# Halved first q*k products, class-1 norms in portions and a reset of the fill model's TensorE position in a fused attention and token-mixing kernel

## Chip, cores, metric

One core of one Trainium2 chip. The metric is the time of one execution on the device in microseconds (us); medians are over several executions. All bf16 data, float32 sums.

## The reference

Two layers, each run twice: A is attention over eight positions two apart, B is a two-matmul mixer over the 2048 tokens.

```python
S, D, H, W, dil, F = 2048, 1024, 32, 8, 2, 3584          # head size 32
def A(x):                                                # x is already layer-normed
    q, k, v = split(x @ wqkv)                            # 32 heads
    idx = pos[:, None] - arange(W) * dil                 # the window: 8 earlier tokens, 2 apart
    attn = softmax(where(idx >= 0, (q * k[idx]).sum(-1) * Dh**-0.5, -1e9))
    return (attn * v[idx]).sum(window) @ wo
def B(x):
    u = gelu(einsum("bsd,sf->bdf", layernorm(x), w1) + b1)
    return transpose(einsum("bdf,fs->bds", u, w2) + b2)
x = x + A(layernorm(x)); x = x + B(layernorm(x))         # and both once more
```

As the window steps by two, even tokens never meet odd ones. The kernel calls them class 0 and class 1 (`c`); each is 1024 tokens, eight tiles of 128 x 1024.

## The kernel before

The q*k products of the window are made on VectorE (`T`), summed over the head by TensorE with a 0/1 matrix (`sel`), turned into probabilities, written to device memory and read back spread over the partitions (`pb`), and multiplied by v on VectorE. Projections, layer norms of the second class and the output projection are "fill" that keeps TensorE busy meanwhile. A small model of TensorE's and VectorE's positions, run while the kernel is built, decides how many fill groups stand between which steps. The engines themselves run their lists in order (run r37_norm0_first below shows it for VectorE). A fill group is eight matmuls of 512 columns, about 1.75 us.

```python
class Attn:
    def weights(self, c, part, dt):          # part 0 q, 1 k, 2 v; loaded when first asked for
        ...                                  # v: two tiles of 512 KB from a pool of five (wb)
                    nc.sync.dma_start(out=t, in_=src)
    def project(self, c, part, dt, hf, ps=None, lo=0, hi=HT):
        ...                                  # 8 matmuls of hi - lo columns, then a ScalarE copy
    def softmax_back(self, n):
        ...                                  # sums, reciprocal, Pb on VectorE
            nc.gpsimd.dma_start(out=dst, in_=Pb[:].rearrange("p u t -> p (u t)"))   # pd, in device memory
            self.spread(n)
    def spread(self, n):
            for hf in range(2):
                ...
                nc.gpsimd.dma_start(out=pb[:].rearrange("p b u t -> p (b u t)"), in_=src)   # 1 MB each

    def stream(self, lead):                  # the main line of one attention layer; weave() adds fill
            for n in range(last + 1):        # n: chunk of 16 heads of one class
                for half in range(2):
                    yield from self.qk(n, 2 * half)
                    yield from self.qk(n, 2 * half + 1)
                    if half:
                        yield from self.softmax_front()
                    ...

def weave(lead, fills, lags):                # pe, dve: modelled positions in us
    ...
            elif kind == "at":
                pe, dve = unit               # sets both positions to given values

def opening():
    for i in range(NT):
        x_stage(0, i)                        # tiles of class 0, alternating between two queues
    load_biases()
    clear_pads()
    with tc.manual_schedule(...):
        first_tiles(hT, ...)                 # norms, transposes and first projections in a fixed order
        for i in range(NT):
            x_stage(1, i)
    yield "at", 27.0, 29.0
    ...
```

## Time and profile before

| | before |
|---|---|
| time, median of 3 (range) | 1280.47 us (1280.17 to 1280.98) |
| profiled span | 1278.8 us |
| TensorE busy | 98% |
| granted TensorE clock | 1.00 |
| start of the first useful projection | 11.98 us |
| start of the value projections after the first softmax | 63.55 us |

```profile
DMA to landing us min/median/max: 4.9/4.9/4.9
```

### The profile page before, as it was taken

The page shows a single profiled execution, that of the slowest core. Times are in us where ns is not written, and L with a number is a line of the kernel's source. Part 1 is how long each engine was busy: PE and PEld are TensorE (multiplying, and loading weights), DVE is VectorE, ACT ScalarE, POOL GpSimd, SP SyncE. Part 2 cuts the span into 40 slices and gives each one's busy share as a digit, 9 for nine tenths or more (in the row PEclk, how much of TensorE's full clock was granted, in tenths as well). Part 3 has the DMA queues.
Part 4 walks back from the last instruction along what each step waited for, and adds up shares of the span by engine and source line. Part 5 has one row for each costly group of instructions (what it writes and reads, how often), then busy time and mean ns, then how long its engine had stood idle before and what let it go on. Part 6 is the DMA issues. An engine that isn't in the chain of part 4 may idle for free.

```text
span 1278.8 us, 15455 instructions
## 1 busy us (share of the span) xinstructions
PE 1258.0 (98%) x6163; PEld 577.4 (45%) x6284; DVE 689.9 (54%) x869; ACT 489.3 (38%) x812; POOL 61.3 (5%) x166
## 2 busy tenths in 40 slices
PE   8999999999999999999999999999999999999998
PEld 4344444444444444444444444444444444444444
DVE  6789999999114322334798834899930233111011
ACT  6845446634424533324533445453352343000000
POOL 3000000001000000000000000010010000000000
PEclk9999999999999999999999999999999999999999
DMA  9853454553422289952738542358262223344331
GB/s 256 190 124 106 99 139 142 171 143 115 132 83 83 64 220 305 291 161 87 187 103 201 152 124 80 83 159 207 66 181 83 82 67 89 107 128 135 99 115 52
DMA packets 217817, 173.00 MB, mean 135 GB/s; under 512 B 32081, under 2 KB 198353, under 8 KB 215697
## 3 DMA queue, kind: packets, MB, share of 16 engines
q1 hardware_dynamic: 206768, 126.11, 36.5%
q0 software_dynamic: 9248, 37.51, 10.5%
q10 hardware_dynamic: 1728, 8.39, 1.7%
q8 instruction: 49, 0.80, 0.3%
q14 instruction: 24, 0.19, 0.0%
HBM read 139.47 MB, written 26.21 MB: 130 GB/s over the span
## 4 chain that ended last, share of the span: by engine, by line
PE 76%; DVE 5%; issue 2%; ACT 1%; DMA 0%; DVEq 0%
PE ps L719 30%; PE ps L743 29%; PE ps L418 11%; PE ps L664 4%; DVE T L456 2%; PE sc L480 1%; DVE pr L538 1%; DVE pr L543 1%; DVE xr L689 0%; ACT h L227 0%; ACT h L238 0%; DMA wo<-in_A_wo_dram 0%; DVE v L545 0%; DVE xr L692 0%; ACT ln L200 0%
## 5 line engine op out<-in xcount | busy, mean ns | idle before, releaser
L719 PE MATMUL ps<-h,w 128*128 128x512 bf16 x1754 | 385.6, 379 | 4.0 <-ACT h L238 2.0
L743 PEld LDWEIGHTS <-w 128*128 128x128 bf16 x1820 | 177.6, 98 | 209.9 <-issue 2.1
L719 PEld LDWEIGHTS <-w 128*128 128x128 bf16 x1792 | 175.2, 98 | 214.1 <-issue 3.4
L418 PE MATMUL ps<-hT,wq 128*128 128x512 bf16 (+1 forms) x1087 | 240.2, 374 | 2.5 <-issue 0.6
L743 PE MATMUL ps<-g,w 128*128 128x512 bf16 (+1 forms) x1017 | 225.9, 376 | 1.2 <-issue 0.2
L743 PE MATMUL ps<-gg,w 128*128 128x512 bf16 (+1 forms) x766 | 170.9, 376 | 0.9 <-issue 0.2
L418 PEld LDWEIGHTS <-wq 128*128 128x128 bf16 x1112 | 109.1, 100 | 128.8 <-issue 9.1
L748 DVE SCALAR_TENSOR_TENSOR xr<-ps,b_sb,xr 128x512 bf16<-128x512 f32 (+1 forms) x65 | 45.5, 738 | 225.1 <-PE ps L743 182.6
L456 DVE TENSOR_TENSOR T<-q,k 128x4096 bf16<-128x4096 bf16 x44 | 99.0, 2284 | 70.5 <-ACT q L422 52.4
L543 DVE TENSOR_TENSOR pr<-pr 128x2048 bf16<-128x2048 bf16 (+1 forms) x128 | 119.4, 949 | 0.3
L730 DVE TENSOR_TENSOR tmp<-ps,gg 128x512 f32<-128x512 f32 x48 | 33.2, 692 | 150.2 <-PE ps L719 148.2
L418 PE MATMUL ps<-hT,wv 128*128 128x512 bf16 x436 | 99.5, 380 | 0.6
L664 PE MATMUL ps<-wo,oT 128*128 128x512 bf16 x377 | 88.6, 379 | 1.1 <-DVE oT L545 0.7
L425 ACT CAST k<-ps 128x1024 bf16<-128x1024 f32 x60 | 60.7, 1014 | 61.0 <-PE ps L418 59.0
L538 DVE TENSOR_TENSOR pr<-pb,v 128x2048 bf16<-128x2048 bf16 x64 | 75.9, 1218 | 10.8 <-ACT v L425 6.1
L538 DVE TENSOR_TENSOR pr<-pb,g 128x2048 bf16<-128x2048 bf16 x64 | 76.6, 1216 | 7.6 <-DMA pb<-pd 5.1
L418 PEld LDWEIGHTS <-wv 128*128 128x128 bf16 x448 | 48.9, 111 | 48.7 <-issue 4.2
L730 DVE TENSOR_TENSOR tmp<-ps,g 128x512 f32<-128x512 f32 x48 | 33.2, 692 | 49.7 <-PE ps L719 46.9
L664 PEld LDWEIGHTS <-oT 128*128 128x128 bf16 x384 | 37.3, 98 | 46.8 <-issue 1.2
L422 ACT CAST q<-ps 128x512 bf16<-128x512 f32 x60 | 34.9, 586 | 49.5 <-PE ps L418 49.5
L731 ACT ACTIVATE gg<-tmp,b_sb 128x512 bf16<-128x512 f32 x48 | 34.6, 721 | 49.9 <-DVE tmp L730 49.9
L731 ACT ACTIVATE g<-tmp,b_sb 128x512 bf16<-128x512 f32 x48 | 34.6, 721 | 43.5 <-DVE tmp L730 43.1
(97 smaller groups left out, 755.9 us busy)
## 6 DMA issues: line engine op xcount, KB each, us to landing
w<-in_B_w_dram SPq DMA_DIRECT2D x56, 512.0 KB, 4.8
w<-in_B_w_dram SPq DMA_DIRECT2D x64, 448.0 KB, 3.8
wq<-in_A_wqkv_dram SPq DMA_DIRECT2D x38, 512.0 KB, 4.3
pb<-pd POOLq DMA_DIRECT2D x16, 1024.0 KB, 8.7
wo<-in_A_wo_dram SPq DMA_DIRECT2D x16, 512.0 KB, 3.9
xa<-xr POOLq DMA_DIRECT2D x32, 256.0 KB, 3.4
xr<-xa SPq DMA_DIRECT2D x32, 256.0 KB, 4.0
wv<-in_A_wqkv_dram SPq DMA_DIRECT2D x14, 512.0 KB, 5.4
```

Source lines behind the costliest of these rows:

```text
L418: nc.tensor.matmul(ps[:, lo:hi], lhsT=cols, rhs=self.hT[c][hf][:, kt, lo:hi], start=(kt == 0), stop=(kt == KD - 1))
L422: nc.scalar.copy(out=self.q_of(c, dt)[:, hf * HT:(hf + 1) * HT], in_=ps[:])
L425: nc.scalar.copy(out=window(buf, 0, PADK + hf * HT, [(KW + 1, 2), (1, HT)]), in_=ps[:].unsqueeze(1).to_broadcast([P, 2, HT]))
L456: mult = nc.vector.tensor_tensor(out=T, in0=q.unsqueeze(1).to_broadcast([P, 4, SC]), in1=window(k, par, 2, [(2, 4), (1, SC)]), op=ALU.mult)
L538: mult = nc.vector.tensor_tensor(out=pr[:, :, u, :], in0=pb[:, :, u, :], in1=window(self.v_of(c, dt), par, 2 + hf * HT, [(TB, 4), (2, 4), ...
L543: nc.vector.tensor_tensor(out=pr[:, :, 0:wd, :], in0=pr[:, :, 0:wd, :], in1=pr[:, :, wd:2 * wd, :], op=ALU.add)
L664: nc.tensor.matmul(banks[(i, n)][:], lhsT=at_.oT[c][kt][:, i * P:(i + 1) * P], rhs=wo_t[n][kt // 4][:, kt % 4, :], start=(kt == 0), stop=( ...
L719: nc.tensor.matmul(ps[:], lhsT=wt[c][:, i, fl * P:(fl + 1) * P], rhs=h2[c][i // 4][:, i % 4, dc * 512:(dc + 1) * 512], start=(k == 0), sto ...
L730: nc.vector.tensor_tensor(out=tmp[:], in0=ps[:], in1=gs, op=ALU.add)
L731: nc.scalar.activation(out=gs, in_=tmp[:], func=ACT.Gelu_apprx_tanh, bias=b1_sb[:, ft:ft + 1])
L743: nc.tensor.matmul(ps[:, 0:xc.stop - xc.start], lhsT=w2t(ft, c), rhs=g[ft // GF][:, ft % GF, xc], start=(ft == 0), stop=(ft == FT - 1))
L748: nc.vector.scalar_tensor_tensor(out=xo[:, xc], in0=ps[:, 0:xc.stop - xc.start], scalar=b2_sb[:, i, c:c + 1], in1=xo[:, xc], op0=ALU.add, ...
```

## The change

The intent is to start useful TensorE work earlier and to have the first q*k sums ready earlier. Tile 0 comes in two halves on two queues; projections start on 128 columns; three q*k products are made on their first half of the tokens before class 1's statistics (`AHEAD_T`); class 1's norms are spread between the products; its last tile moves from ScalarE to VectorE; and as the projections have moved ahead of the first softmax, the model's positions are set anew there (`39.3, 54.6`).

```diff
+    AHEAD_T = ((0, 0), (0, 1), (1, 0))
...                                          # first_tiles: new order of statistics, norms, transposes, projections
+        for dq, par in AHEAD_T:
+            ahead(0, dq, par, HT)
     def prologue_tile(c, i, hT):
         t = staged(c, i)
-        if i % 2:
+        if i % 2 and i < NT - 1:            # this branch normalises on ScalarE
...
             if lead is not None:
-                yield "drain", "second"
+                for dq, par in AHEAD_T:
+                    self.multiply_ahead(0, dq, par, SC)
+                yield from self.qk(0, 0)
+                for u in ((1, 3, 1), (0, 2, 0)):
+                    yield from self.proj(0, *u)
+                self.multiply_ahead(0, 1, 1, SC)
+                for u in ((0, 2, 1), (0, 3, 0), (0, 3, 1)):
+                    yield from self.proj(0, *u)
+                yield "drain", "second", NT // 2
...
+                    if lead is not None and n == 0:
+                        yield "drain", "second", NT // 4
                     if half:
+                        if lead is not None and n == 0:
+                            yield "at", 39.3, 54.6
                         yield from self.softmax_front()
...
         def opening():
-            for i in range(NT):
-                x_stage(0, i)
-            load_biases()
+            x_stage(nc.sync, 0, 0, slice(0, P // 2))
+            x_stage(nc.scalar, 0, 0, slice(P // 2, P))
+            x_stage(nc.scalar, 0, 1)
+            x_stage(nc.sync, 0, 2)
+            at_.weights(0, 1, 0)
+            x_stage(nc.scalar, 0, 3)
+            x_stage(nc.sync, 0, 4)
+            at_.weights(0, 0, 0)
...                                          # biases load after class 1's tiles
```

More of the change, by code (lines that the diff above doesn't have):

```diff
@@ L139 @@
     sel = const.tile([P, SB * DQ, 32], BF16, name="sel")
+    maskc = const.tile([P, W, W], FP32, name="maskc")
+    b1_bf = const.tile([P, FT], BF16, name="b1_bf")
+    b2_bf = const.tile([P, NT, DIL], BF16, name="b2_bf")
+    b1_sb = const.tile([P, FT], FP32, name="b1_sb")
+    b2_sb = const.tile([P, NT, DIL], FP32, name="b2_sb")
     nc.gpsimd.memset(sel[:], 0.0)
@@ L145 @@
                 nc.gpsimd.memset(sel[hp * DH:(hp + 1) * DH, sb * DQ + dq, col:col + 1], 1.0)
-    maskc = const.tile([P, W, W], FP32, name="maskc")
     nc.gpsimd.memset(maskc[0:CH], 0.0)
@@ L150 @@
             nc.gpsimd.memset(maskc[0:CH, s, 0:w], NEG)
-    b1_bf = const.tile([P, FT], BF16, name="b1_bf")
-    b2_bf = const.tile([P, NT, DIL], BF16, name="b2_bf")
-    b1_sb = const.tile([P, FT], FP32, name="b1_sb")
-    b2_sb = const.tile([P, NT, DIL], FP32, name="b2_sb")
     def load_biases():
@@ L245, in staged, with x_stage, first_tiles @@
         return g[n // GF][:, n % GF, :]
-    def x_stage(c, i):
-        eng = nc.gpsimd if c else (nc.scalar if i % 2 else nc.sync)
-        eng.dma_start(out=staged(c, i), in_=xin_v[c, i])
-    def first_tiles(hT, project):
+    def x_stage(eng, c, i, part=slice(0, P)):
+        eng.dma_start(out=staged(c, i)[part], in_=xin_v[c, i][part])
+    def first_tiles(hT, project, ahead):
         tiles = [staged(0, i) for i in range(NT)]
-        mv, rs, tps = {}, {}, {}
+        bn, mv, rs, tps = {}, {}, {}, {}
         s1, t1, nm, ss = (st(n, [P, w]) for n, w in (("s1", NDC), ("t1", 1), ("nm", 1), ("ss", 1)))
@@ L262, in idle, with stats, root, moments @@
                                  rhs=ident[:].unsqueeze(1).to_broadcast([P, 4, P]), start=True, stop=True)
-        def moments(i):
-            s = st("bn", [P, NDC, 6])
-            for n in range(NDC):
-                nc.vector.bn_stats(out=s[:, n, :], in_=tiles[i][:, n * 512:(n + 1) * 512])
-            mv[i] = st("mv", [P, 2])
-            nc.vector.bn_aggr(out=mv[i][:], in_=s[:])
+        def stats(i, n):
+            if n == 0:
+                bn[i] = st("bn", [P, NDC, 6])
+            nc.vector.bn_stats(out=bn[i][:, n, :], in_=tiles[i][:, n * 512:(n + 1) * 512])
+            if n == NDC - 1:
+                mv[i] = st("mv", [P, 2])
+                nc.vector.bn_aggr(out=mv[i][:], in_=bn[i][:])
+        def root(i):
             rs[i] = st("rs", [P, 1])
             rsqrt(rs[i][:], mv[i][:, 1:2], 1.0, eps1)
+        def moments(i):
+            for n in range(NDC):
+                stats(i, n)
+            root(i)
         def norm(i):
@@ L295, in first_tiles @@
         dve, act = nc.vector.tensor_copy, nc.scalar.copy
-        idle(16)
-        moments(0)
-        own_sum(0)
-        moments(1)
+        idle(14)
+        stats(0, 0)
+        stats(0, 1)
+        root(0)
+        stats(1, 0)
         norm(0)
         turn(0)
+        stats(1, 1)
+        root(1)
+        place(0, act)
+        own_sum(0)
         idle(3)
-        own_sum(1)
-        moments(2)
+        stats(2, 0)
         norm(1)
         turn(1)
-        idle(5)
-        place(0, act)
@@ L309, in first_tiles @@
-        moments(3)
-        place(1, dve)
-        norm(2)
-        norm(3)
-        banks = {}
-        for u, i in (((1, 0), 2), ((1, 1), 3), ((0, 0), None)):
-            banks[u] = bank()
-            project(*u, 0, banks[u], 0, 2 * P)
-            if i:
-                turn(i)
-        own_square()
-        place(2, act)
+        banks = {u: bank() for u in ((1, 0), (1, 1), (0, 0), (0, 1))}
+        for u in ((1, 0), (1, 1)):
+            project(*u, 0, banks[u], 0, P)
+        stats(2, 1)
@@ L321, in first_tiles @@
+        root(2)
+        place(1, act)
+        stats(3, 0)
+        norm(2)
+        turn(2)
+        stats(3, 1)
+        root(3)
+        own_sum(1)
+        own_square()
+        norm_act(tiles[own], tiles[own], nm, rs[own])
+        place(2, dve)
+        for u in ((1, 0), (1, 1)):
+            project(*u, 0, banks[u], P, 2 * P)
+        norm(3)
+        project(0, 0, 0, banks[(0, 0)], 0, 2 * P)
+        turn(3)
+        stats(own + 1, 0)
         place(3, dve)
-        norm_act(tiles[own], tiles[own], nm, rs[own])
@@ L323, in first_tiles @@
-        moments(own + 1)
+        project(0, 1, 0, banks[(0, 1)], 0, 2 * P)
+        stats(own + 1, 1)
+        root(own + 1)
         moments(own + 2)
+        norm(own + 1)
         for n, u in enumerate(banks):
             project(*u, 0, banks[u], 2 * P, HT)
-            if n == 0:
+            if n == 2:
                 turn(own)
-                norm(own + 1)
                 place(own, dve)
-                moments(own + 3)
-                norm(own + 2)
-        for n, u in enumerate(((0, 1), (1, 2), (1, 3))):
-            if n == 2:
-                norm(own + 3)
-            turn(own + 1 + n)
-            place(own + 1 + n, dve)
-            project(*u, 0, bank(), 0, HT)
@@ L339, in first_tiles @@
-        for u in ((1, 0), (1, 1), (0, 0), (0, 1)):
+        moments(own + 3)
+        norm(own + 2)
+        turn(own + 1)
+        place(own + 1, dve)
+        norm(own + 3)
+        project(1, 2, 0, bank(), 0, HT)
+        turn(own + 2)
+        place(own + 2, dve)
+        ps = bank()
+        project(1, 3, 0, ps, 0, 2 * P)
+        turn(own + 3)
+        place(own + 3, dve)
+        project(1, 3, 0, ps, 2 * P, HT)
+        for u in ((1, 0), (0, 0), (1, 1), (0, 1)):
             project(*u, 1, bank(), 0, HT)
+        for dq, par in AHEAD_T:
+            ahead(0, dq, par, HT)
@@ L364, in __init__ @@
             self.prior = None
+            self.begun = {}
         def v_of(self, c, dt):
@@ L417, in project @@
                     cols = wt[0][:, kt, (dt % 2) * P:(dt % 2 + 1) * P]
-                nc.tensor.matmul(ps[:, lo:hi], lhsT=cols, rhs=self.hT[c][hf][:, kt, lo:hi], start=(kt == 0), stop=(kt == KD - 1))
+                self.last_mm = nc.tensor.matmul(ps[:, lo:hi], lhsT=cols, rhs=self.hT[c][hf][:, kt, lo:hi], start=(kt == 0), stop=(kt == KD - 1))
             if hi < HT:
@@ L454, in qk @@
                     yield "pe", 0.6, [], [], 0.0
-                T = self.t_buf(n, dq, par)
-                mult = nc.vector.tensor_tensor(out=T, in0=q.unsqueeze(1).to_broadcast([P, 4, SC]),
-                                               in1=window(k, par, 2, [(2, 4), (1, SC)]), op=ALU.mult)
+                if (n, dq, par) in self.begun:
+                    self.multiply_ahead(n, dq, par, SC)
+                    T, _, mult = self.begun[(n, dq, par)]
+                else:
+                    T = self.t_buf(n, dq, par)
+                    mult = self.multiply(T, q, k, par, 0, SC)
                 Ts.append(T)
@@ L462, in qk @@
                 if not joined:
-                    self.qk_sum(dq, par, T)
+                    mms = self.qk_sum(dq, par, T)
+                    if dq == 1 and par:
+                        follow(mms[0], self.last_mm, mybir.DependencyClass.NoSync)
             if joined:
@@ L468, in qk, with multiply, multiply_ahead @@
                     follow(x, y, mybir.DependencyClass.NoSync)
+        def multiply(self, T, q, k, par, lo, hi):
+            return nc.vector.tensor_tensor(out=T[:, :, lo:hi], in0=q[:, lo:hi].unsqueeze(1).to_broadcast([P, 4, hi - lo]),
+                                           in1=window(k, par, 2 + lo, [(2, 4), (1, hi - lo)]), op=ALU.mult)
+        def multiply_ahead(self, n, dq, par, hi):
+            c, dt = n // NCQ, (n % NCQ) * DQ + dq
+            T, lo, mult = self.begun.get((n, dq, par)) or (self.t_buf(n, dq, par), 0, None)
+            if lo < hi:
+                mult = self.multiply(T, self.q_of(c, dt), self.k_of(c, dt), par, lo, hi)
+            self.begun[(n, dq, par)] = T, hi, mult
         def t_buf(self, n, dq, par):
+            if (self.li, n, dq, par) == (0, 0, 1, 0):
+                return g_two[-1][:].rearrange("p (u t) -> p u t", u=4)
             if self.li == 0 and 0 < n < 3:
@@ L595, in stream @@
                     turn = nx == (NCQ, 0) and self.li > 0
-                    yield from self.qk(n, 2 * half)
+                    if lead is None or n or half:
+                        yield from self.qk(n, 2 * half)
                     yield from self.qk(n, 2 * half + 1)
+                    if lead is not None and n == 0:
+                        yield "drain", "second", NT // 4
                     if half:
+                        if lead is not None and n == 0:
+                            yield "at", 39.3, 54.6
                         yield from self.softmax_front()
-                    if lead is not None and nx == (0, 1):
-                        for u in ((0, 2, 1), (0, 3, 0), (0, 3, 1),):
-                            yield from self.proj(0, *u)
-                    elif nx[0] <= last and not turn:
+                    if nx[0] <= last and not turn and (lead is None or nx != (0, 1)):
                         yield from qk_proj(*nx)
@@ L832, in weave @@
             elif kind == "drain":
-                while unit[0] in opened:
+                for _ in range(unit[1]) if unit[1:] else iter(int, 1):
+                    if unit[0] not in opened:
+                        break
                     pull(True)
@@ L871, in opening @@
         def opening():
-            for i in range(NT):
-                x_stage(0, i)
-            load_biases()
+            x_stage(nc.sync, 0, 0, slice(0, P // 2))
[6 more added lines that the diff above has]
+            at_.weights(0, 0, 0)
+            for i in range(5, NT):
+                x_stage(nc.sync, 0, i)
             clear_pads()
             with tc.manual_schedule(engines={getattr(mybir.EngineType, e) for e in ("PE", "DVE", "Activation", "Pool")}):
-                first_tiles(hT, partial(at_.project, 0))
+                first_tiles(hT, partial(at_.project, 0), at_.multiply_ahead)
                 for i in range(NT):
-                    x_stage(1, i)
+                    x_stage(nc.gpsimd, 1, i)
+                load_biases()
             yield "at", 27.0, 29.0
-            for u in ((1, 2, 1), (1, 3, 1), (0, 2, 0),):
-                yield from at_.proj(0, *u)
+            yield from at_.proj(0, 1, 2, 1)
         def second_class():
```

## The prediction

> **What bounds the kernel now.** I first read the page's busy row, then the chain that ended last, then TensorE's own waits, then the first 64 us engine by engine in order of time.
>
> ```profile
> PE 1258.0 (98%) x6163; PEld 577.4 (45%) x6284; DVE 689.9 (54%) x869; ACT 489.3 (38%) x812; POOL 61.3 (5%) x166
> PE 76%; DVE 5%; issue 2%; ACT 1%; DMA 0%; DVEq 0%
> PE sc L480 <- DVE T L456: 3.4, 9, 1.2
> PE ps L719 <- ACT h L238: 2.0, 2, 1.2
> PE tp L290 <- DVE gg L233: 1.8, 2, 1.2
> ```
>
> TensorE is busy 98% of 1278.8 us and carries 76% of the chain; its named waits sum to about 11 us (the three largest shown: total us, times, longest). So a change outside the matmuls themselves can win a few us at most. The diff touches only the first softmax and what precedes it, so that is where I look:
>
> ```profile
> 1.57 5.30 PE L261 MATMUL ps<-ident 128*128 128x512 bf16 x16 [1.57 <-POOL ident masks.py:199]
> 8.06 0.62 PE L290 MATMUL tp<-ident,gg 128*128 128x128 bf16 x8 [1.19 <-DVE gg L233]
> 8.52 0.81 PE L261 MATMUL ps<-ident 128*128 128x512 bf16 x3
> 9.90 0.62 PE L290 MATMUL tp<-ident,gg 128*128 128x128 bf16 x8 [0.57 <-DVE gg L233]
> 10.36 1.24 PE L261 MATMUL ps<-ident 128*128 128x512 bf16 x5
> 11.98 1.03 PE L418 MATMUL ps<-hT,wq 128*128 128x256 bf16 x8 [0.38 <-ACT t L281]
> ...
> 25.61 7.07 PE L418 MATMUL ps<-hT,wq 128*128 128x512 bf16 x31
> ...
> 39.65 0.61 PE L480 MATMUL sc<-T,sel 128*32 128x512 bf16 x8 [1.24 <-DVE T L456]
> ```
>
> Columns: start, duration, engine, line, what; idle before it in brackets. The 24 products on `ident` compute nothing: they fill time and keep the array's clock up. The first useful projection starts at 11.98. From there to 25.61 TensorE has no gap worth naming (13.47 busy of 13.63). One more gap, 1.24 us, comes at the first q*k sum, which waits for VectorE's product T. Counting the stretch 25.61 to 63.55 (start of the value projections after the first softmax's sums): 144 matmuls of 512 columns at 0.217 (56 of them ran in the 12.19 us to 37.80) are 31.2, 64 sum matmuls at 0.069 (16 take 1.1) are 4.4; 37.9 less 35.6 leaves 2.3 us of stalls.
>
> **What the Trainium skill says.** "TensorE: Matmul & The Clock Gate", section "Wait — 56ns, not 53.3ns?": start-to-start 55.6 ns for 128 columns and 215.7 for 512 when warm, twice that cold. The trace agrees: eight transposes start 0.46 us ahead of what follows (57 ns each), the long stretches run at 217 ns. Sixteen `ident` products took 5.30 us, which solves to about nine cold; so fourteen of them still pass the warm-up, and I expect no cold projections. "VectorE: DVE Perf Modes", section "The perf-mode tier table": a bf16 tensor_tensor of 2048 elements takes 1224 ns. The trace agrees (1218 for 2048, 2284 for 4096); two halves of T cost 0.1 us more than one whole. "DMA: Bandwidth & Descriptors", section "Anatomy of one DMA — SWDGE (gpsimd) path": about 2.0 us fixed plus the bytes. Here a 256 KB tile lands 3.1 us after issue when the engines are free, and 5 to 6 in a crowd. The same page, section "Issuing engines are not separate DMA queues": splitting a load over queues saves only issue time, so halving tile 0 helps only because tile 1 no longer shares its first microsecond.
>
> **The change, part by part.** Durations are from the trace of before; in-order positions are from the built instruction lists of both kernels. All clock times of the new kernel are estimates.
>
> Loading. Tiles 0 and 1 landed at 4.6 to 4.8, when about 0.7 MB had moved. With tile 0 in two halves at the head of two queues, it needs 0.26 MB, which had moved by about 3.1; with the same 0.8 from there to the landing, it lands near 3.95. The first weights move from fifth to third on their queue: 1.5 MB ahead of or beside them at 0.33 MB/us gives 7.5 instead of 10.9.
>
> Tile 0. Two statistics (1.32) and the aggregate (0.2) end at 5.5, the root on ScalarE (0.56) at 6.05. VectorE now does one half of tile 1's statistics, not both and the aggregate, ahead of the normalisation: 6.05 to 6.55 instead of 7.47 to 8.01. Turn 0 starts at 6.6 (was 8.06); fourteen fillers, at 2 x 0.22 less, end at 6.4.
> Tile 1. Statistics end 7.35, root 7.9, normalised 8.45, turn 1 at 8.5 to 8.95 (was 9.90). ScalarE copies hT of tile 0 from 7.9 to 8.85 (was 9.91 to 10.9).
> First projection: 8.95, on 128 columns of tile 0, against 11.98. The five last fillers (1.24) are gone. But turn 2 must wait for tile 2's root, which stands behind the hT copy and a sum on ScalarE: 10.5, while the two 128-column groups end at 9.9. So 0.6 us of the 3.0 is given back. Then hT of tile 1 (10.95), tile 2 (11.85), tile 3 (14.1) and the ScalarE-normalised tile 4 (16.0) are each ready as TensorE arrives; the rest of the opening has the same columns as before. I place the start of the second-half projections at 23.05 against 25.61: 2.55 us won.
>
> Class 1. Its loads are triggered by the last transpose, so they start 1.3 us earlier in the trace's terms (24.35 becomes 23.05), land from 26.15, and no longer meet the two bias loads, which before had the DMA engines over 90% busy at under 100 GB/s about 12 to 15 us. VectorE, in order, does one T half (22.95 to 24.1), then waits for that first tile.
> VectorE from 26.15 without a gap: statistics 1.32, four T halves 4 x 1.14, aggregate and statistics 1.4, half 1.14, whole T 2.22 (ends 36.85); then normalisations of tiles 0, 2 and 4, statistics of tiles 4 and 6, and half of tile 7, which is new on VectorE: 4.9; T of the next channel at 41.8 to 44.05, the remaining tile 7 statistics 0.77, three more T to 51.4.
> TensorE: 80 matmuls and 16 sums from 23.05 reach 41.45, two sum groups 42.55; the next sum waits for 44.05 (1.5 us), the later three wait 0.45, 0.15 and 0.15. That is 2.25 us of stalls, as many as before: the stall moves from one place to another. Sums end at 52.0 (was 59.0), and the value projections start at 61.0 against 63.55. Won: 2.55.
>
> After that. VectorE runs the softmax and the next products some 7 us earlier, TensorE 2.55. From 63.55 to 188 TensorE had no wait, and the reset of the fill model shifts only one or two fill groups between the same waits; total columns are equal. At 188.1 the output projection waited 0.67 for VectorE, at 200.2 a sum 0.3, at 230.8 ScalarE's normalised tile 1.17. VectorE's lead should remove the first and perhaps half of the other two: 1.4 less. From 240 on both kernels are the same and TensorE-bound.
> Sum: 2.55 + 1.4 = 3.95. I hold back 0.75 for waits I have not seen, since every step above sits on hand-placed starts: 3.2 won, 1280.47 - 3.2 = 1277.3.
>
> **Rivals.**
> (a) The VectorE chain is worse than counted. Tile 7's work (2 statistics, aggregate, normalisation: 1.9 us) moves to VectorE ahead of the sums, and VectorE is full from 26 to 51. For it: three sums in a row stand with nothing between them on TensorE. If class-1 tiles land 2 us late (they took up to 6.1 before), TensorE waits 3.5 instead of 1.5 there; 1279.3. Against: they now meet less traffic.
> (b) Tile 0 does not land sooner, because halves of a tile share the same 16 engines. Then all of the opening shifts by 0.65: 1278.0.
> (c) Waits after 188 all vanish and VectorE's lead stays: 2.1 instead of 1.4, nothing held back; 1275.8.
> (d) The opening's gain is eaten wholly by later waits on VectorE, which is 93% busy from 63.55 to 188 and could set the pace there: 1280. Against it: VectorE starts that stretch earlier than TensorE does, and TensorE shows no wait in it.
>
> **Range and chances.** 1275.3 to 1279.3 covers (a) to (c), each alone. The three runs of before lie within 0.8 us. Two per cent is 25.6 us: more than all of TensorE's idle time together, and no step I found could cost as much. Faster 0.005, same 0.99, slower 0.005.
>
> **What would show it right or wrong.** In the changed kernel: tile 0's statistics start near 3.95; first projection near 9.0, with some 0.6 idle ahead of turn 2; second-half projections near 23; the largest wait of the stretch, about 1.5, ahead of the fifth sum group (T on the next channel); last sum near 52; value projections at 61. If the last sum ends near 52 but the end gains nothing, (d) holds. If the fifth sum waits over 3, (a) holds. If I am wrong beyond the range, it will be through a DMA wait in the opening (the second weights, estimated 10.5 to 11 for a need at 11.9) or a fill placed so that the first softmax's ScalarE copy comes late.

## More of the kernel before

A 512 KB load of value weights goes out on the SyncE queue as soon as TensorE has finished with the buffer that it fills, and 1 MB loads of spread probabilities go out on the GpSimd queue. First SyncE's queue, then GpSimd's, in order of time (start and duration of the issue; the bracket is what the issue waited for):

```profile
122.68 0.37 SPq L396 DMA_DIRECT2D wv<-in_A_wqkv_dram  x1
123.54 0.67 SPq L654 DMA_DIRECT2D wo<-in_A_wo_dram  x1
```

```profile
119.20 0.63 POOL L506 DMA_DIRECT2D pd<-Pb  x1 [45.35 <-DVE Pb L502]
124.58 0.51 POOL L520 DMA_DIRECT2D pb<-pd  x1 [4.75 <-DVE pr L538]
130.16 0.51 POOL L520 DMA_DIRECT2D pb<-pd  x1 [5.07 <-DVE pr L538]
```

The weights leave 1.90 us ahead of the first `pb`. TensorE's timeline runs through this stretch without a bracket:

```profile
121.62 15.70 PE L418 MATMUL ps<-hT,wv 128*128 128x512 bf16 x70
```

The weights on tile `wv` took 4.9 us (the line on DMA in this section), so they landed at 127.6.

## The result and the profile after

The changed kernel took 1287.40 us (median of 6, 1283.02 to 1290.54), against 1280.53 (1280.17 to 1281.08) for the kernel before beside it: 6.9 us slower where 3.2 faster was predicted. The ratio is 1.005, with an interval of 1.0033 to 1.0068.

The busy row and the chain, which the prediction read first, hardly move:

```profile
PE 1259.1 (98%) x6188; PEld 579.6 (45%) x6309; DVE 692.4 (54%) x876; ACT 487.1 (38%) x802; POOL 61.5 (5%) x166
PE 75%; DVE 5%; issue 2%; ACT 1%; DMA 0%; DVEq 0%
```

TensorE's waits do (total us, times, longest). The first line is new:

```profile
PE ps L447 <- DMA wv<-in_A_wqkv_dram: 6.4, 1, 6.4
PE sc L527 <- DVE T L505: 4.3, 11, 0.9
```

The opening on TensorE, in order of time; it answers to the timeline in the prediction. "Turn 0" in the prediction and below is its first line, the eight transposes of tile 0; turn 1 is those of tile 1:

```profile
8.21 0.62 PE L299 MATMUL tp<-ident,gg 128*128 128x128 bf16 x8 [0.72 <-DVE gg L235]
...
10.66 1.06 PE L447 MATMUL ps<-hT,wq 128*128 128x128 bf16 x16
...
24.64 7.08 PE L447 MATMUL ps<-hT,wq 128*128 128x512 bf16 x31
...
45.05 0.62 PE L527 MATMUL sc<-T,sel 128*32 128x512 bf16 x8 [0.91 <-DVE T L505]
...
61.86 4.48 PE L447 MATMUL ps<-hT,wv 128*128 128x512 bf16 x19
```

The first projection is 1.3 us earlier, the second-half projections 1.0 earlier, the value projections 63.55 - 61.86 = 1.7 earlier. So the opening does win, though less than predicted. Then TensorE stands at 126:

```profile
118.03 7.93 PE L447 MATMUL ps<-hT,wv 128*128 128x512 bf16 x35
132.31 11.89 PE L447 MATMUL ps<-hT,wv 128*128 128x512 bf16 x43 [6.35 <-DMA wv<-in_A_wqkv_dram]
```

SyncE's queue and GpSimd's at the same place, and the landing time of these weights:

```profile
120.81 0.37 SPq L425 DMA_DIRECT2D wv<-in_A_wqkv_dram  x1
121.67 0.61 SPq L711 DMA_DIRECT2D wo<-in_A_wo_dram  x1
```

```profile
115.61 0.63 POOL L553 DMA_DIRECT2D pd<-Pb  x1 [46.90 <-DVE Pb L549]
121.24 0.51 POOL L567 DMA_DIRECT2D pb<-pd  x1 [5.00 <-DVE pr L585]
126.57 0.51 POOL L567 DMA_DIRECT2D pb<-pd  x1 [4.82 <-DVE pr L585]
```

```profile
DMA to landing us min/median/max: 11.5/11.5/11.5
```

The same 512 KB took 11.5 us instead of 4.9. Its issue comes 1.9 us earlier than before, but the first `pb` comes 3.3 earlier, so the lead shrank from 1.90 to 0.43 us. The need came sooner too: TensorE stood 5.15 us after the issue (125.96 - 120.81). Two runs below that have the fill order of the kernel before, r37_x_first and r37_norm0_first, show when it would have come there: TensorE began its wait for these weights 6.87 and 6.88 us after their issue. So two things got worse at once, and both come from where the fill stands.

The profile also tells whose packets the 16 engines moved from 124 to 128 us: q0 carries GpSimd's loads (`pb`), q1 SyncE's (the value weights and the loads around them); the columns are packets, MB and share of the engines' time. First the changed kernel, then the one before:

```profile
q0 software_dynamic: 110, 0.88, 100.0%
q1 hardware_dynamic: 32, 0.03, 4.0%
```

```profile
q1 hardware_dynamic: 1617, 1.31, 103.1%
q0 software_dynamic: 7, 0.06, 4.0%
```

In the changed kernel the `pb` load had the engines almost to itself while the weights were still missing. Before, the weights' queue had them, and `pb` came after.

There is a second cost. Windows over the stall, after (busy us of each engine, then the granted clock, DMA share, GB/s):

```profile
126.00:130.00 4.00, 0.00 (x0) 0.00 (x0) 4.00 (x4) 0.15 (x1) 0.51 (x1) 1.00 1.02 237
130.00:132.00 2.00, 0.00 (x0) 0.00 (x0) 2.00 (x2) 0.00 (x0) 0.00 (x0) 0.50 1.15 256
132.00:134.00 2.00, 1.69 (x4) 0.59 (x5) 2.00 (x2) 0.00 (x0) 0.00 (x0) 0.50 1.04 220
134.00:136.00 2.00, 2.00 (x6) 0.73 (x5) 0.95 (x2) 1.02 (x1) 0.00 (x0) 0.50 0.32 71
136.00:138.00 2.00, 2.00 (x9) 0.87 (x8) 0.00 (x0) 0.61 (x1) 0.00 (x0) 0.79 0.04 16
138.00:140.00 2.00, 2.00 (x11) 1.08 (x10) 0.00 (x0) 1.29 (x2) 0.00 (x0) 1.00 0.00 0
```

The array's clock halved while it stood, and came back after 136. That is as the Trainium skill has it ("TensorE: Matmul & The Clock Gate", section "What's actually happening"): half rate after an idle window of about 3.4 us, and full rate again after about as long of work. Here it halved 4.0 us into the wait (at 130.0) and was back 4.5 us after the work began (at 136.8). The 43 matmuls after the stall took 11.89 us; the run pb_late below did 44 there in 9.69, of which one matmul is 0.2, so the cold clock cost about 2.4.

The sum: 6.35 + 2.4 - 1.7 = 7.05 us slower. The second part of the output projection starts at 221.20 us, before at 214.13: 7.07 later. The spans differ by 6.7, the medians by 6.9; at 746 us the kernel before idles 0.44 for no wait that the profile shows, and the changed one does not. So the stall and its cold clock account for the loss to within 0.4 us.

### The profile page after: what moved, and what is told of

Same layout as the page of the kernel before. It is cut to its first block, busy times and chain, and to the rows that moved or that the text cites. A ratio compares the mean times of both kernels' runs of the same rounds, so it can differ in the third digit from the quotient of the medians. Undisturbed runs are those within 1.5% of the kernel's fastest.

```text
span 1285.5 us, 15502 instructions
## 1 busy us (share of the span) xinstructions
PE 1259.1 (98%) x6188; PEld 579.6 (45%) x6309; DVE 692.4 (54%) x876; ACT 487.1 (38%) x802; POOL 61.5 (5%) x166
## 4 chain that ended last, share of the span: by engine, by line
PE 75%; DVE 5%; issue 2%; ACT 1%; DMA 0%; DVEq 0%
PE ps L776 29%; PE ps L800 29%; PE ps L447 11%; PE ps L721 4%; DVE T L505 2%; PE sc L527 1%; DVE pr L585 1%; DVE pr L590 1%; DVE xr L746 1%; ACT h L229 0%; ACT h L240 0%; DMA hT<-hb 0%; DVE xr L749 0%; ACT ln L202 0%; DVE v L592 0%
## 5 line engine op out<-in xcount | busy, mean ns | idle before, releaser
L447 PE MATMUL ps<-hT,wq 128*128 128x512 bf16 (+2 forms) x1112 | 239.8, 370 | 1.8 <-issue 0.3
L505 DVE TENSOR_TENSOR T<-q,k 128x4096 bf16<-128x4096 bf16 (+1 forms) x45 | 97.2, 2193 | 70.4 <-ACT q L451 52.0
L447 PE MATMUL ps<-hT,wv 128*128 128x512 bf16 (+1 forms) x443 | 101.6, 382 | 6.9 <-DMA wv<-in_A_wqkv_dram 6.4
```

Of the source, the lines that this page charges most:

```text
L447: self.last_mm = nc.tensor.matmul(ps[:, lo:hi], lhsT=cols, rhs=self.hT[c][hf][:, kt, lo:hi], start=(kt == 0), stop=(kt == KD - 1))
L505: return nc.vector.tensor_tensor(out=T[:, :, lo:hi], in0=q[:, lo:hi].unsqueeze(1).to_broadcast([P, 4, hi - lo]), in1=window(k, par, 2 + lo ...
```

## Experiments

**1. pb_late: take the collision away.** The changed kernel, with the two `pb` loads of that chunk held until the value weights have landed.

```diff
-            self.spread(n)
+            if (self.li, n) != (0, 1):
+                self.spread(n)
...
-                nc.gpsimd.dma_start(out=pb[:].rearrange("p b u t -> p (b u t)"), in_=src)
+                pb_load = nc.gpsimd.dma_start(out=pb[:].rearrange("p b u t -> p (b u t)"), in_=src)
+                if load:
+                    follow(pb_load, load, mybir.DependencyClass.Sync)
...
+                        if (self.li, n) == (0, 1):       # after the value projections' weights are asked for
+                            self.spread(n, self.last_load)
```

> The changed kernel, where only the two loads of the spread probabilities of the second chunk (2 MB in all) wait until the value weights that TensorE stalled on at 125.9 us have landed; every engine's list is otherwise the same. Theory 1, the two loads share the 16 DMA engines and the probabilities squeeze the weights: issued at 120.8, the weights land in 4 to 5 us as in the kernel before, the 6.35 us stall and the half-clock stretch after it go, span about 1285.5 - 6.4 - 2.2 = 1277, time 1278 to 1279, steady to 1 us. Theory 2, the fill order releases and uses that weight buffer too close together, whatever else is in flight: the stall stays at 4 us or more and the time above 1283.

Measured: 1279.56 us (1279.02 to 1280.12), ratio to before 0.9988 [0.9973, 1.0002], so 7.8 us under the changed kernel. The `pb` loads now go out at 127.28, the weights take 6.2 us, and the stall is down to what the early need leaves (5.16 us after the issue):

```profile
126.78 9.69 PE L447 MATMUL ps<-hT,wv 128*128 128x512 bf16 x44 [1.10 <-DMA wv<-in_A_wqkv_dram]
185.73 11.40 PE L726 MATMUL ps<-wo,oT 128*128 128x512 bf16 x52 [0.87 <-DVE oT L595]
```

The collision is the cause of the stall, all but the 1.10 us that the early need leaves. Holding the probabilities back 6 us brought no other new wait.

**2. reset37: move the model's position alone.** `"at", 39.3, 54.6` becomes `"at", 37.6, 54.6`. The built lists then have the fill order of the kernel before from the first softmax on.

> The changed kernel with the fill model's TensorE position set to 37.6 instead of 39.3, one fill unit (1.75 us) earlier, which gives TensorE the fill order of the kernel before from the first softmax on. Theory 1 (collision, set by how far VectorE leads and by the lead time from release to use): use comes 1.5 us later after release, so the stall shrinks but does not vanish unless the probability loads also come later; 0 to 4.5 us, time 1278.5 to 1285. Theory 2 (fill order alone): no stall, time 1278 to 1279.

Measured: 1280.28 us (1279.90 to 1281.47), ratio 0.9995 [0.998, 1.001]. The weights go out at 121.94, 1.56 ahead of `pb`, land 6.2 later, and there is no stall. So a shift of 1.7 us in a number that only places fill is worth 7 us here.

**3. no_reset: the changed kernel without the reset.**

```diff
-                        if lead is not None and n == 0:
-                            yield "at", 39.3, 54.6
```

> The changed kernel without the reset of the fill model's position. The model then believes TensorE to be later and puts fewer class-1 value units early, so that some are left behind the third softmax and the output projection is split around the sums. If the reset is what brings the weights' release and use together, the 6.35 us stall is gone; but TensorE waits longer for VectorE before the output projection and after it, by 2 to 5 us: 1280 to 1285. If the reset does not matter, the stall and about 1287 stay.

Measured: 1285.92 us (1282.61 to 1286.62), ratio 1.0036 [1.0019, 1.0053]. The weights' stall is 0.29, but other waits come up, by TensorE's timeline:

```profile
97.02 1.05 PE L527 MATMUL sc<-gg,sel 128*32 128x512 bf16 x16 [1.38 <-DVE gg L505]
101.42 1.05 PE L527 MATMUL sc<-gg,sel 128*32 128x512 bf16 x16 [1.29 <-DVE gg L505]
133.96 2.78 PE L447 MATMUL ps<-hT,wv 128*128 128x512 bf16 x12 [0.29 <-DMA wv<-in_A_wqkv_dram]
191.83 3.78 PE L719 MATMUL ps<-wo,oT 128*128 128x512 bf16 x10 [2.61 <-DMA wo<-in_A_wo_dram]
```

After the last of these the granted clock was 0.50 from 192.5 to 195.9 us. A reset is needed, then; it is its value that put the fill in a bad place. The first `pb` load went out 6.04 us ahead of the weights here (119.66 and 125.70), and the weights took 8.2 us; the stall is small only because the need, too, came 8 us after the issue. So going out behind `pb` is slow as well.

**4. before_collide and before_collide2: bring the collision into the kernel before.** The weights' load is made to wait, first for a VectorE product, then for the landing of the write of `pd`.

```diff
+                    load = nc.sync.dma_start(out=t, in_=src)
+                    if (self.li, key, n) == (0, (0, 2, 1), 1):
+                        follow(load, self.pb_free, mybir.DependencyClass.Sync)    # before_collide
+                        follow(load, self.pd_write, mybir.DependencyClass.Sync)   # before_collide2
```

> The kernel before, where the same value weights wait for the VectorE product that also releases the first probability load, so that they are issued together at 124.5 instead of 1.9 us ahead of it. Theory 1: the weights land some 11 us later, at about 135.5 to 136, TensorE stalls 6 us from 129.5 and runs some us at half clock; time 1286 to 1290. Theory 2: they land in 5 us, at 129.4, just in time; time within 1 us of the kernel before.

Measured: 1280.32 us (1280.09 to 1280.57), ratio 0.9993 [0.9979, 1.0008]. A miss of the experiment: the product was done before the wait could hold anything, the weights went out at 122.84 against `pb` at 124.61. It tells nothing.

> The kernel before, where the value weights that it loads at 122.7 us wait for the landing of the probabilities' write, which is what the first probability load of the second chunk waits for too; so both are issued together near 124.6 (the earlier try at this missed: its wait was over before it bit, and the weights still led by 1.8 us). TensorE needs them near 129.5. Collision theory: they land 10 to 11.5 us after issue, at 135 to 136, TensorE stalls 5.5 to 6.5 us and then runs some 4 us at half clock; 1286 to 1290. Fill-order theory (the lead time from release to use, 5 us, is what matters): they land in 5 to 6 us, stall 0 to 1 us, time within 1.5 us of the kernel before.

Measured: executions of 1280.46, 1287.70, 1289.46 and 1287.86 us, ratio 1.0047 [1.0018, 1.0075]. The profile caught the 1280.46: weights out at 124.07, `pb` at 124.61, landing after 5.6 us, no stall. In the other three the kernel before is as slow as the changed one. So one program falls either way; its lead was 0.54 us in the execution that got off free, and is not known for the others. That the slow three stalled as in the changed kernel is inferred from their time and from the granted clock (0.997, as in the changed kernel, against 1.00); no trace shows it.

**5. pb_2k: smaller rows.** I suspected that the `pb` load's rows of 8 KB starve the weights' rows of 1 KB. The Trainium skill ("DMA: Bandwidth & Descriptors", section "Queues, rings and completion order") says that each DMA engine goes round the queues and drains a whole packet of one before the next. Each `pb` load of that chunk becomes four with rows of 2 KB.

```diff
+                parts = 4 if (self.li, n) == (0, 1) else 1
+                for m in range(parts):
+                    size = 4 * W * TB // parts
...
+                    nc.gpsimd.dma_start(out=pb[:].rearrange("p b u t -> p (b u t)")[:, m * size:(m + 1) * size], in_=src)
```

> The changed kernel with each of the two probability loads of the second chunk issued as four, of 2 KB rows instead of 8 KB rows; same bytes. If a row of one queue is taken in turn with a row of the other, weights of 1 KB rows get a third of the engines instead of a ninth: they land in about 5 to 7 us instead of 11.5, the stall falls from 6.35 to under 2 us and the clock is not lost; time 1278 to 1281. If the engines are shared by bytes, or the loads are simply too many, the stall stays about 6 us and the time about 1287.

Measured: 1284.37 us (1281.98 to 1289.04), ratio 1.0019 [1.0, 1.0037]; in the profiled execution (the slowest) the weights took 10.6 us and TensorE stalled 5.53. That landing and that stall fit the second theory, but the share of the engines fits the first: q1, the weights' queue, had 30.9% of the engines' time from 125 to 129 us, near the third reckoned with, against the 4.0% above. And the lead was 0.01 us here, not 0.43. So smaller rows gave the weights more of the engines but did not save this landing; what they would do at the same lead is not shown, and the other three executions (1281.98 to 1285.41) have no trace. The rate fell as well, from 344 and 340 GB/s (124 to 126, 126 to 128 us) before to 236 and 222 in the changed kernel, at a DMA share above 1.0 in both. That is the rate of the `pb` load itself: alone on the engines in the kernel before, from 130 to 134 us, it moved 0.89 MB, 222 GB/s, at a share of 100.0%.

**6. r37_x_first: is the opening short because of the load order?** On top of reset37, the first weights go behind tiles 2 and 4 on their queue.

```diff
-            at_.weights(0, 1, 0)
             x_stage(nc.scalar, 0, 3)
             x_stage(nc.sync, 0, 4)
+            at_.weights(0, 1, 0)
             at_.weights(0, 0, 0)
```

> The changed kernel with the fill position at 37.6 and, in the opening, the first two weight loads behind tiles 2 and 4 on their queue instead of between them; all engine lists but the DMA queue's are as in the run with 37.6 alone. Theory: turn 0 starts at 8.2 to 9.0 instead of the predicted 6.6 because VectorE stands, in order, at tile 1's statistics until tile 1 lands at 7.0, its rows being shared with the weights' 512-byte rows. Then tile 1 lands near 5, turn 0 starts near 6.9, the first projection near 9.2 and the end gains 1.0 to 1.5 us on 37.6 alone: about 1279. Rival: the first megabyte simply moves more slowly whatever its order; turn 0 stays over 8 and the time within 0.5 of 37.6 alone.

Measured: 1280.97 us (1279.74 to 1283.07), ratio 1.0006 [0.9991, 1.0021]. Turn 0 came at 9.14, tile 1 landed at 7.9, no better than reset37 (8.52 and 7.3). The order is not it.

**7. r37_x_first_tile7: the last class-1 tile back on ScalarE** (`if i % 2:`), on top of run 6.

> The same with tile 7 of class 1 normalised on ScalarE as in the kernel before. Theory: the 1.3 to 1.9 us of VectorE work ahead of the third channel's product is what TensorE waits for at the fifth sum group (0.9 to 1.7 us there); without it that wait falls by 0.6 to 1.3 us, and the end gains as much if no other wait takes its place. Rival: the product then waits for ScalarE's copy of the projection, since ScalarE has the tile's three passes (3 us) back; the wait stays.

Measured: 1279.28 us (1278.43 to 1286.61), ratio 1.0004 [0.9976, 1.0031]. The fifth sum waits 1.97 (1.74 in reset37), but the 0.34 at the sixth is gone, and three of the four executions are 1278.4 to 1279.5. The fourth, 1286.61, has the size of the stall, although the profiled execution issued the weights 1.94 us ahead of `pb` (landing after 6.6 us). If it was that, and no trace shows it, fill order alone does not make the kernel safe.

**8. r37_whole: tile 0 in one piece again**, on top of reset37.

```diff
-            x_stage(nc.sync, 0, 0, slice(0, P // 2))
-            x_stage(nc.scalar, 0, 0, slice(P // 2, P))
+            x_stage(nc.sync, 0, 0)
             x_stage(nc.scalar, 0, 1)
```

> The fill reset at 37.6, and tile 0 loaded whole again on one queue, tile 1 at the head of the other, as the kernel before does; the rest of the change stays. If the two half-tile issues ahead of tile 1 are what makes tile 1 land at 7 us: tile 0 lands near 4.6, tile 1 near 4.9, turn 0 near 7.4 (8.5 with the halves), the first projection near 9.9 (11.0), and the time falls by 0.3 to 1.1 us, to 1279.2 to 1280.0, less if VectorE's products at the fifth sum swallow it. If the first megabyte is slow whatever the issue: tile 1 again at 6.5 to 8, turn 0 at 8.3 to 8.8, time 1280.3.

Measured: 1278.91 us (1278.26 to 1281.96), ratio 0.9991 [0.9976, 1.0007]. Turn 0 comes at 7.29, 1.2 us earlier than with the halves. VectorE's opening in the changed kernel, then in this one:

```profile
4.29 1.29 DVE L268 BATCH_NORM_STATS2 bn<-gg 128x6 f32<-128x512 bf16 x2 [3.39 <-DMA gg<-in_A_x_dram]
5.61 0.21 DVE L271 BATCH_NORM_AGGREGATE mv<-bn 128x2 f32<-128x12 f32 x1
7.01 0.69 DVE L268 BATCH_NORM_STATS2 bn<-gg 128x6 f32<-128x512 bf16 x1 [1.20 <-DMA gg<-in_A_x_dram]
7.62 0.53 DVE L235 TENSOR_SCALAR gg<-gg,mv,rs 128x1024 bf16<-128x1024 bf16 x1
```

```profile
4.55 1.29 DVE L268 BATCH_NORM_STATS2 bn<-gg 128x6 f32<-128x512 bf16 x2 [3.65 <-DMA gg<-in_A_x_dram]
5.87 0.21 DVE L271 BATCH_NORM_AGGREGATE mv<-bn 128x2 f32<-128x12 f32 x1
6.00 0.64 DVE L268 BATCH_NORM_STATS2 bn<-gg 128x6 f32<-128x512 bf16 x1
6.68 0.55 DVE L235 TENSOR_SCALAR gg<-gg,mv,rs 128x1024 bf16<-128x1024 bf16 x1
```

The halves bring tile 0 by 0.26 us and cost tile 1 over a microsecond: VectorE, in order, stands at tile 1's statistics with tile 0 ready to be normalised. DMA work from 3 to 6 us, changed kernel and then this one (last columns: clock, DMA share, GB/s):

```profile
3.00:6.00 3.00, 3.00 (x9) 1.03 (x7) 1.50 (x3) 0.15 (x1) 2.15 (x26) 1.00 1.00 250
```

```profile
3.00:6.00 3.00, 3.00 (x9) 1.06 (x7) 1.41 (x4) 0.00 (x0) 2.15 (x26) 1.00 0.99 346
```

As busy, but at 250 GB/s against 346. The eight kernels with the halves moved 249 to 300 there, the six without them 331 to 352.

**9. r37_norm0_first: keep the halves, normalise tile 0 before tile 1's statistics**, on top of reset37.

```diff
-        stats(1, 0)
         norm(0)
+        stats(1, 0)
```

> The fill reset at 37.6, halves of tile 0 kept, but VectorE normalises tile 0 before it takes tile 1's first statistics. If VectorE, in order, standing at tile 1's statistics is what holds turn 0: turn 0 near 7.1 (8.5), turn 1 near 10.0 (10.5), first projection near 10.45 (10.97). Time lower by 0 to 0.5 us. If something else holds it (the root on ScalarE, the fillers): turn 0 stays at 8.2 to 8.6.

Measured: 1280.54 us (1278.71 to 1281.32), ratio 0.9996 [0.9983, 1.001]. Turn 0 came at 7.06 and turn 1 at 9.63, so it was the order on VectorE that held turn 0. The time gained nothing measurable: the profiled execution has a wait of 0.9 for the value weights again.

**10. best and best_no_halves: everything together, and the halved products priced.** `best` is the changed kernel with the late `pb` loads of run 1, 37.6, tile 0 whole, and tile 7 on ScalarE. `best_no_halves` also lacks the three products ahead of class 1's statistics:

```diff
-        for dq, par in AHEAD_T:
-            ahead(0, dq, par, HT)
```

> Everything that the runs so far speak for together: spread-probability loads held until the value weights have landed, fill reset at 37.6, tile 0 whole, tile 7 of class 1 on ScalarE as in the kernel before. If the collision of the two loads is the cause of the whole loss, no execution falls into the stall and the gain of the opening shows: 1278.3 to 1279.3 in all executions, about 1.5 us under the kernel before. If the late spread loads cost something of their own: 1280 or more, with a wait at the attention products.

Measured: 1278.37 us (1277.66 to 1280.18, five executions) against 1280.66 (1280.44 to 1281.33, nine) for before: ratio 0.9983 [0.997, 0.9995]. It is 2.3 us faster: small, but the interval leaves 1 out, and no execution has the size of a stall. "In all executions" was a little too much: one of the five took 1280.18. Lines of its opening on TensorE, to be read against those of the changed kernel, then the `pb` loads that wait for the weights:

```profile
9.75 1.06 PE L447 MATMUL ps<-hT,wq 128*128 128x128 bf16 x16
...
44.33 0.61 PE L527 MATMUL sc<-T,sel 128*32 128x512 bf16 x8 [1.10 <-DVE T L505]
...
60.66 5.56 PE L447 MATMUL ps<-hT,wv 128*128 128x512 bf16 x24
```

```profile
126.70 1.02 POOL L568 DMA_DIRECT2D pb<-pd  x2 [9.94 <-DMA wv<-in_A_wqkv_dram]
```

The value projections start 63.55 - 60.66 = 2.9 us earlier than in the kernel before, and 2.4 of them reach the end of the span (1276.4 against 1278.8); at 554 us best idles 0.94 for no wait that the profile shows.

> The kernel of the run named best without the three halved products ahead of the first class-1 statistics. It prices the halves. If they use VectorE time that is idle otherwise (about 1.1 us before the first class-1 tile lands, and fewer products behind the second halves of q and k), the fifth sum waits 1 to 2 us longer and the time is 1 to 1.5 us above best. If the sums do not hang on them: within 0.3 us of best.

Measured: 1280.27 us (1278.15 to 1280.59, five), ratio 0.9991 [0.9978, 1.0003]. The first two sums wait instead of the fifth:

```profile
33.52 0.62 PE L525 MATMUL sc<-T,sel 128*32 128x512 bf16 x8 [0.88 <-DVE T L503]
35.72 0.85 PE L525 MATMUL sc<-T,sel 128*32 128x512 bf16 x8 [1.58 <-DVE T L503]
```

Its value projections start at 63.90 against 60.66, 3.2 us later. Of these 0.88 + 1.58 - 1.10 = 1.36 are the waits themselves. Most of the rest is the clock: after these two waits it was granted at 0.50 from 36.0 to 39.4 us, which costs half of 3.4. At the end 2.2 us of span remain, since best's 0.94 at 554 us is not there. But the profile caught the slowest execution. The five fall in two groups: 1280.27 to 1280.59 with a granted clock of 0.999, and 1278.15 and 1278.47 with 1.00, about as fast as four of best's five (1277.66 to 1278.39). So what the halves save seems to be mostly the halving of the clock, some 2 us in the executions that have it (one is traced, the others are judged by the clock); where the clock holds, no gain is shown, and no trace of such an execution was kept. The mean times differ by 1.0, and against the kernel before this one's interval includes 1.

## Why the prediction was wrong

**The step that failed.** "From 63.55 to 188 TensorE had no wait, and the reset of the fill model shifts only one or two fill groups between the same waits; total columns are equal." The count was right: the reset moves about that many groups. The conclusion was not. A fill group sets when a weight buffer comes free and when its next content is needed, and so when a load goes out and what it meets. I had looked for waits in the kernel before, found none, and took that for slack; I did not ask how far each load's landing lay ahead of its first use (here 127.6 against an estimated 122.7 + 6.9 = 129.6: 2.0 us). The runs put in its place a stall of 6.35 us with 2.4 us of cold clock after it (after, pb_late, reset37), and before_collide2 shows that the kernel before can be made to lose the same 7 us (three executions of four).

**Other steps.**
- *Tile 0 at 3.95, turn 0 at 6.6, first projection at 8.95.* They came at 4.29, 8.21 and 10.66. I had reckoned that tile 0 alone sets turn 0, but put tile 1's first statistics ahead of tile 0's norm without asking when tile 1 lands. It landed at 7.0. r37_whole and r37_norm0_first show both halves of this. The fourteen fillers, too, ended at 7.49, not 6.4, so turn 0 at 6.6 was out of reach in this execution; in best it stands straight behind them, at 7.33. Over the runs with fourteen they end between 6.2 and 7.5. Rival (b) had the direction, but 0.65 for the 1.6 that came.
- *Second-half projections at 23.05, 2.55 won.* They came at 24.64, 0.97 won, the same 1.6 late as turn 0: everything from the first projection on took the time predicted. In best they came at 23.73, and its value projections 2.9 us ahead of the kernel before's, where 2.55 was predicted.
- *The fifth sum waits 1.5.* It waited 0.91, and 1.10 to 2.11 in the kernels with the halved products and without the stall: right that VectorE's products set the pace there. The product that it waits for ended at 45.0, not 44.05; the sums ended at 53.0 (52.0 predicted), and the value projections started at 61.86 (61.0).
- *1.4 us of later waits removed.* The wait at the output projection was 0.67 and became 0.87, the 0.30 stayed, and the 1.17 for ScalarE went, but a sum near it then waited 0.88 for VectorE: nothing to speak of. In best they are 0.68, 0.30 and 1.17, although there all else went well. VectorE's lead does not last that long: the first probabilities were written out 5.8 us earlier than before (62.48 against 68.29), the second 3.6 (115.61 against 119.20), no more than TensorE's own lead at that place (118.03 against 121.62). This term should have been zero.
- *What would make it wrong.* I named DMA waits, but only in the opening, and a badly placed fill, but only for the first softmax's copy. None of the four rivals had a transfer that another transfer delays in the middle of the kernel.
- *Same within 2%.* Right; but the range of 4 us was drawn from waits visible before, and a load that lands 2 us ahead of its need was not among them.

## What to carry to other kernels

Before moving fill on a saturated engine, list every load whose buffer that fill frees or whose content it needs, with its landing and its first use; where the distance is a couple of microseconds, the move is a change to that load, however few groups it shifts. Make a load that TensorE will stand for go ahead of bulk loads by a dependency, as in pb_late and best, rather than by where the schedule happens to put it. And on an engine that runs in order, a sooner transfer helps only if nothing ahead of its user waits for a later one.

## What the Trainium skill lacked or had wrong

- "DMA: Bandwidth & Descriptors", section "Anatomy of one DMA — SWDGE (gpsimd) path": a fixed time plus the bytes, for a load that GpSimd issues. No page gives the landing in company. The same 512 KB of weights, issued by SyncE, took 5.9 to 6.5 us with the 1 MB loads held back, 4.9 to 7.7 with the first of them 1.56 to 2.20 us behind, 5.6 with it 0.54 behind, and 11.5 with it 0.43 behind.
- The same page, section "Queues, rings and completion order": it has turns by packet, but not how the engines' time is divided when one queue's rows are eight times as long. From 124 to 128 us the queue with 8 KB rows had 100.0% of it and the one with 1 KB rows 4.0%, 110 packets to 32; with rows of 2 KB in place of 8 KB the weights' queue had 30.9%. One program (before_collide2) took 1280.5 or 1287.7 to 1289.5 us; the page has nothing on this.
- The same page, section "Issuing engines are not separate DMA queues": says that issuing on several engines saves only issue time, and its rules for kernel authors call two partition halves not worth the bother. It lacks that this can cost: with a tile halved over two queues, 249 to 300 GB/s were moved from 3 to 6 us in place of 331 to 352, and the next tile landed over 1 us later.
- "TensorE: Matmul & The Clock Gate", section "What's actually happening": the stall of 6.35 us agrees, but its idle window of about 3.4 us is no safe measure of a single wait. The clock was also halved, for 3.4 us each time, after one wait of 2.61 us (no_reset) and after two of 0.88 and 1.58 with eight sums between them (best_no_halves).
